# The second MLP's two products formed from seven block products each, in two stages with a*b kept in DRAM

## The chip, the cores and the metric

The kernel runs on one core of a Trainium2 chip. The metric is the device time of one execution in microseconds (us); lower is better. The engines are named as in the profile: PE (TensorE matmuls), PEld (its weight loads), DVE (VectorE), ACT (ScalarE), POOL (GpSimd), SP (the queue that issues the DMAs).

## The reference

Attention over 4 batches of 544 positions (32 global, 512 local, a window of 32) gives `x` with 2176 rows of 512. Two MLPs follow. This is the part that counts here:

```python
def _moe_ref(x, w_in, w_out):            # w_in 512 x 2048, w_out 2048 x 512
    h = np.maximum(x @ w_in, 0.0)
    return (h * h @ w_out).astype(np.float32)

def _moe2_ref(x, w1, w2, w3, w_out):     # w1, w2 512 x 1024, w3 1024 x 1024, w_out 1024 x 512
    a = x @ w1
    b = x @ w2
    h = a * b @ w3
    return (h @ w_out).astype(np.float32)
```

All arrays are float64 or float32 on the way in, and every matrix product has to be near float32 accuracy.

## The kernel before

**Products.** Activations lie with features on the 128 partitions and positions along the columns. A product near float32 is made of three passes of the reduced type `float32r`: an operand is split into a high part (a cast on ACT) and a low part (`raw - high`, `split_lo`, line 106), and `PASSES` multiplies high by high, high by low and low by high. So each raw operand tile costs one ACT instruction and one two-input DVE instruction before PE can use it. On DVE both inputs of `split_lo` lie in SBUF.

**Weights.** The inputs come as 64-bit floats, taken apart as integers. `conv(n)` makes unit n (128 x 512) of the 72: a 512 KB DMA (`load_w`), two ACT instructions (lines 373, 376), two DVE instructions (lines 381, 386), one POOL add (line 396), then the split. The calls `keep_in_program_order` hold the first ACT and the first DVE instruction of each unit at their place in the program.

**Order.** The text of the kernel is a program order. A planner with a model of the engines then fixes each engine's own order; a tile that has a tag and `bufs` waits for a free slot of that tag. `merge` spreads filler steps (the weights) between the main steps.

**Stages.** First attention with the first half of the first MLP, then its second half (`rows(NBLK + i, 16, 24, ...)`, eight blocks of 256 and 288 columns), with the weights of the second MLP as filler. In it `w_unit` also forms `w3 @ w_out` of the second MLP, kept in DRAM as `w_d`, so that the second MLP is `(a * b) @ w_d`. Its input `x2` is stored to DRAM (`x2_d`) block by block. The last stage is the second MLP: five blocks of columns, one of 256 and four of 480. For each block `p_unit` makes `a` and `b` for one of eight groups f of 128 features (24 matmuls), multiplies them (line 682) and splits the result at once; `x_add` adds group f's part to four accumulators (12 matmuls). A block so takes 8 x 36 = 288 matmuls; `end_c` copies the four results out and stores them.

Of the kernel before, what the change touches and what calls it, by code (L numbers as in the profile page):

```python
# [74 lines left out]
def attention_mlp(ctx: ExitStack, tc: tile.TileContext, kq0, kq, vw, wts, mask, ident, out):  # L75
# [569 lines left out]
    big = (NT - HALF) // 4
    blocks = [(0, HALF)] + [(HALF + big * k, big) for k in range(4)]
    x2, wv = {}, {}  # L650

    def load_x2(i):
        if i < len(blocks):
            s, n = blocks[i]
            x2[i] = sb.tile([128, 4, big], F32, tag="xb", name="x2l", bufs=2)[:, :, :n]
            nc.sync.dma_start(out=x2[i], in_=x2_d[:, :, s : s + n])

    def parts_c(n):
        return parts(n) if n <= NB else u2.tile([128, 2, big], F32R, tag="vb", name="hl_c", bufs=8)

    def split_x2(i, k):
        if i < len(blocks):
# [115 lines left out]
```

## Time and profile before

| | |
|---|---|
| device time, median of 3 runs | 901.23 us (900.71 to 902.02) |
| span of the profiled execution | 901.2 us |
| granted TensorE clock, mean over the span | 0.996 of full speed |
| PE busy | 869.4 us (96%) |
| DVE, ACT, POOL busy | 451.2, 473.7 and 164.8 us |
| HBM read and written | 71.63 and 19.92 MB |

The span is the time from the first to the last instruction of one profiled execution. "Busy" is the time in which an engine had an instruction running; PE's ends are modelled, so that rates of matmuls are better taken from how far apart their starts lie. POOL's busy time includes time in which it waits inside an instruction.

### The profile page before, as it was taken

To read this page: it belongs to the slowest core of one execution; us is meant where nothing else is said; L and a number is where in the kernel's file an instruction comes from. 1 tells how busy PE (TensorE), PEld (TensorE's weight loads), DVE (VectorE), ACT (ScalarE), POOL (GpSimd) and SP (SyncE) were. 2 spreads that over 40 slices of the span, in tenths; PEclk is the share of its full clock that TensorE was granted. 3 is DMA by queue.
4 is the path that set the end of the run, shared out by engine and by line. 5 is a ranking of instruction groups with operands and counts; after the bars stand their busy time and mean duration, and the time that the engine had idled before them with its cause. 6 is when DMAs were issued, how large, how long until landed. Compare 5 with 4: busy or idle time off the path is not lost.

```text
span 901.2 us, 15879 instructions
## 1 busy us (share of the span) xinstructions
PE 869.4 (96%) x6088; PEld 790.0 (88%) x6088; DVE 451.2 (50%) x1247; ACT 473.7 (53%) x1219; POOL 164.8 (18%) x182
## 2 busy tenths in 40 slices
PE   5798999999999999999999999999999999999998
PEld 3577898899999999999988999999988888888886
DVE  6998776876485455668545556753100200202101
ACT  5887675666476577878556576853111211212211
POOL 1442000000020022222222212211111111111111
PEclk9999999999999999999999999999999999999999
DMA  6653424313133055455353635544000200100101
GB/s 233 208 172 86 133 77 125 99 55 117 51 95 120 1 170 189 148 187 183 132 198 117 196 105 168 192 141 159 24 1 1 88 0 1 44 1 1 44 1 44
DMA packets 52348, 92.59 MB, mean 103 GB/s; under 512 B 4400, under 2 KB 35248, under 8 KB 52272
## 3 DMA queue, kind: packets, MB, share of 16 engines
q1 hardware_dynamic: 52272, 91.57, 30.9%
q8 instruction: 48, 0.79, 0.4%
q14 instruction: 28, 0.23, 0.1%
HBM read 71.63 MB, written 19.92 MB: 102 GB/s over the span
## 4 chain that ended last, share of the span: by engine, by line
PE 65%; DMA 13%; ACT 11%; DVE 8%; issue 2%; POOL 1%; SPq 1%; ACTq 0%; POOLq 0%; DVEq 0%
PE ab L117 21%; PE acc L468 14%; DMA wraw<-in_wts 12%; PE h L117 11%; PE x L117 8%; PE o L111 3%; PE sc L111 3%; ACT wt L373 3%; PE tp L265 3%; ACT wt L376 2%; DVE wt L386 2%; POOL wt L396 1%; PE sg L117 1%; ACT r L432 1%; DVE p L184 1%
## 5 line engine op out<-in xcount | busy, mean ns | idle before, releaser
L396 POOL TENSOR_TENSOR wt<-wt 128x512 int32<-128x512 int32 x72 | 97.4, 1352 | 294.8 <-DVE wt L386 214.0
L682 DVE TENSOR_TENSOR r<-r,ab 128x480 f32<-128x480 f32 (+1 forms) x40 | 24.3, 607 | 220.0 <-PE ab L117 219.2
L117 PE MATMUL h<-hl,ua 128*128 128x256 f32 (+1 forms) x768 | 120.1, 297 | 1.7 <-ACT hl L422 0.7
L117 PE MATMUL h<-hl,va 128*128 128x256 f32 (+1 forms) x768 | 111.0, 289 | 1.5 <-ACT r L432 1.4
L468 PE MATMUL acc<-hl,vb 128*128 128x256 f32 (+1 forms) x768 | 110.7, 289 | 1.7 <-DVE hl L106 1.6
L117 PEld LDWEIGHTS h<-hl,ua 128*128 128x128 f32 x768 | 103.4, 190 | 7.1 <-issue 1.7
L468 PEld LDWEIGHTS acc<-hl,vb 128*128 128x128 f32 x768 | 102.4, 188 | 4.2 <-DVE hl L106 2.2
L117 PEld LDWEIGHTS h<-hl,va 128*128 128x128 f32 x768 | 102.3, 188 | 3.4 <-ACT r L432 2.4
L117 PE MATMUL x<-hl,ub 128*128 128x288 f32 (+1 forms) x576 | 89.9, 296 | 1.4 <-ACT ub L397 1.2
L468 PE MATMUL acc<-hl_c,wv 128*128 128x480 f32 x384 | 89.2, 380 | 0.0
L117 PE MATMUL ab<-hl_c,ua 128*128 128x480 f32 x384 | 87.1, 380 | 0.0
L117 PE MATMUL ab<-hl_c,ub 128*128 128x480 f32 x384 | 86.6, 380 | 0.0
L117 PEld LDWEIGHTS ab<-hl_c,ub 128*128 128x128 f32 x384 | 72.0, 188 | 11.9
L117 PEld LDWEIGHTS ab<-hl_c,ua 128*128 128x128 f32 x384 | 71.9, 188 | 11.9
L117 PEld LDWEIGHTS x<-hl,ub 128*128 128x128 f32 x576 | 77.1, 189 | 5.8 <-issue 2.5
L468 PEld LDWEIGHTS acc<-hl_c,wv 128*128 128x128 f32 x384 | 72.1, 188 | 11.3
L681 ACT COPY r<-ab 128x480 f32<-128x480 f32 (+1 forms) x40 | 20.9, 523 | 116.2 <-PE ab L117 113.9
L106 DVE TENSOR_TENSOR hl<-r,hl 128x288 fp32r<-128x288 f32 (+1 forms) x128 | 69.6, 547 | 21.1 <-ACT r L439 19.9
L373 ACT ACTIVATE wt<-wraw 128x512 f32<-128x512 f32 x72 | 48.5, 675 | 58.8 <-DMA wraw<-in_wts 55.4
L106 POOL TENSOR_TENSOR hl_c<-r,hl_c 128x480 fp32r<-128x480 f32 x32 | 39.2, 1225 | 210.7 <-ACT hl_c L684 203.0
L188 ACT ACTIVATE p<-p,st 128x256 f32<-128x256 f32 x128 | 64.4, 509 | 7.0 <-DVE st L184 6.9
L684 ACT CAST hl_c<-r 128x480 fp32r<-128x480 f32 x32 | 19.0, 594 | 84.3 <-DVE r L682 84.3
(92 smaller groups left out, 1313.4 us busy)
## 6 DMA issues: line engine op xcount, KB each, us to landing
wraw<-in_wts SPq DMA_DIRECT2D x72, 512.0 KB, 3.4
v_f<-in_vw SPq DMA_DIRECT2D x24, 256.0 KB, 2.8
x2l<-x_d SPq DMA_DIRECT2D x4, 960.0 KB, 5.7
out<-y SPq DMA_DIRECT2D x16, 240.0 KB, 2.3
kqraw<-in_kq SPq DMA_DIRECT2D x24, 144.0 KB, 2.9
x_d<-xb SPq DMA_DIRECT2D x4, 576.0 KB, 6.0
part_d<-st SPq DMA_DIRECT2D x4, 576.0 KB, 3.3
xl<-x_d SPq DMA_DIRECT2D x4, 576.0 KB, 5.4
```

The source lines that it names most:

```text
L106: eng.tensor_tensor(out=lo, in0=raw, in1=hi.bitcast(F32), op=ALU.subtract)
L111: m = mm(o, w, x, start=start, stop=stop)
L117: mm(o, w, x, start=(k == 0), stop=(k == len(terms) - 1))
L188: nc.scalar.activation(p[:, n, :], p[:, n, :], AF.Exp, bias=least[:, n : n + 1], scale=-1.0, accum_out=sums[:, n, 0:1],)
L265: nc.tensor.transpose(tp[:, k, :], p[:, t % 2, 128 * half : 128 * (half + 1)], ident_sb)
L373: first = nc.scalar.activation(t[0].bitcast(F32), raw[:, :, 1].bitcast(F32), AF.Copy, scale=2.0**-112)
L376: nc.scalar.activation(t[2], raw[:, :, 0].bitcast(U32), AF.Copy, scale=2.0**-29)
L396: nc.gpsimd.tensor_tensor(out=b, in0=b, in1=m, op=ALU.add)
L468: mm(acc[d], w[:, a, 128 * d : 128 * (d + 1)], g_t[f][:, b], start=(f + k == 0), stop=(f + k == 9),)
L681: nc.scalar.copy(r, a)
L682: nc.vector.tensor_tensor(out=r, in0=r, in1=b, op=ALU.mult)
L684: nc.scalar.copy(g[:, 0], r)
```

## The change

The columns are cut into four panels p of 544 (two halves of `NP` = 272). A product of 2 x 2 blocks is made of seven block products in place of eight, with sums and differences of blocks formed before and after (Strassen's algorithm in Winograd's form). `ORDER` is the order of the seven, `BANK` the accumulator of each: 7 is added onto 6, 2 onto 1, 3 onto 5.

For `a` and `b` the blocks of the weights are w1 and w2 by halves of the 512 input features, those of the other operand are halves of the features by halves of the columns. `combine` makes the seven weight operands of a group f: four POOL sums of 256 columns and three and a half splits. `operands` makes those of a panel: four POOL sums of 544 elements for each raw tile, and 14 splits of 272 columns (28 for the second product). `Blocks.step` runs one product and what evacuates it: a copy on ACT and DVE sums that read PSUM. `ab_unit` is one panel and group: 7 x 6 matmuls of 272 columns, one DVE and one POOL multiplication, and a store of a*b to `r_d` in DRAM.

When all four panels have been through this, the second stage loads `r_d` panel by panel: two raw tiles, in the two slots of tag `xb`, by four DMAs. `y_unit` runs 7 x 12 matmuls of 272 columns for one of two pairs of output groups. The operands of panel p + 1 are made between the products of panel p.

Sixteen slots `u1` and sixteen `u2` take the place of the old tags. Groups f 0 to 3 lie in `u1` and are made in the first MLP's last stage; the weights of f 4 to 7 (`conv` 64 to 71, with their `combine`) are now made in the first 36 steps of the new stage. In the last panel the groups run in the order 4 to 7, 0 to 3, and the weights of the second product (`combine(("v", j), ...)`) are made beside the last four. `HL_BUFS` is 14 (13 before).

```diff
-UNITS = ["ua"] * 8 + ["ub"] * 8 + ["va"] * 8 + ["vb"] * 8 + ["ub"] * 8 + ["ua"] * 16 + ["ua"] * 8 + ["ub"] * 8
-
-RUNS = (0, 16, len(UNITS))
+UNITS = ["u1"] * 16 + ["u2"] * 16 + ["u1"] * 24
+PAIRED = len(UNITS)
+RUNS = (0, 16, PAIRED + 8, PAIRED + 16)
+
+
+
+ORDER = (1, 6, 5, 7, 4, 2, 3)
+BANK = {1: 0, 6: 1, 5: 2, 7: 1, 4: 3, 2: 0, 3: 2}
+NP = S // 2
...
-AT_BUFS, H_BUFS, X_BUFS, P_BUFS, KQ_BUFS, ST_BUFS = 4, 2, 2, 5, 4, 6
+AT_BUFS, H_BUFS, X_BUFS, P_BUFS, KQ_BUFS, ST_BUFS, HL_BUFS = 4, 2, 2, 5, 4, 6, 14
...
+    r_d = dram.tile([128, 8, NT], F32, name="r_d")
...
+    def unit(tag, dtype=F32R):
+        return pools[tag].tile([128, 2, 512], dtype, tag=tag, name=tag, bufs=16)
+
+    def split_w(t, cols, raw):
+        nc.scalar.copy(t[:, 0, cols], raw)
+        split_lo(nc.vector, t[:, 1, cols], raw, t[:, 0, cols])
+
+    blocks_w, both_t, half_t = {}, {}, {}
+
+    def combine(key, n, tag):
+
+        x = both_t.pop(key)
+        a11, a12, a21, a22 = (x[:, m, 256 * k : 256 * (k + 1)] for m in range(2) for k in range(2))
+        s = unit(tag, F32).rearrange("p a c -> p (a c)")
+        s1, s2, s3, s4 = (s[:, 256 * k : 256 * (k + 1)] for k in range(4))
+        p, q, r = (unit(tag) for _ in range(3))
+        add = nc.gpsimd.tensor_tensor
+        split_w(p, slice(0, 512), x[:, 0])
+        add(out=s1, in0=a21, in1=a22, op=ALU.add)
+        add(out=s2, in0=s1, in1=a11, op=ALU.subtract)
+        split_w(q, slice(0, 512), s[:, :512])
+        add(out=s3, in0=a11, in1=a21, op=ALU.subtract)
+        add(out=s4, in0=a12, in1=s2, op=ALU.subtract)
+        split_w(r, slice(0, 512), s[:, 512:])
+        if n % 2 == 0:
+            half_t[tag] = unit(tag)
+        h, at = half_t[tag], 256 * (n % 2)
+        split_w(h, slice(at, at + 256), a22)
+        blocks_w[key] = {1: (p, 0), 2: (p, 256), 5: (q, 0), 6: (q, 256), 7: (r, 0), 3: (r, 256), 4: (h, at)}
...
     def conv_c(n):
         _, b, m = mid_t.pop(n)
-        tag = UNITS[n]
-        t = pools[tag].tile([128, 2, 512], F32R, tag=tag, name=tag, bufs=8)
+        if n >= PAIRED:
+            f, u = divmod(n - PAIRED, 2)
+            tag = "u1" if f < 4 else "u2"
+            if u == 0:
+                both_t[f] = unit(tag, F32)
+            nc.gpsimd.tensor_tensor(out=both_t[f][:, u].bitcast(I32), in0=b, in1=m, op=ALU.add)
+            if u == 1:
+                combine(f, f, tag)
+            return
         nc.gpsimd.tensor_tensor(out=b, in0=b, in1=m, op=ALU.add)
...
+        t = w_t[n] = unit(UNITS[n])
+        split_w(t, slice(0, 512), b.bitcast(F32))
...
+    def banks():
+        return [
+            ps.tile([128, 512], F32, tag=tag, name="m", bufs=bufs)[:, :NP]
+            for tag, bufs in (("h", H_BUFS), ("at", AT_BUFS), ("at", AT_BUFS), ("x", X_BUFS))
+        ]
+
+    def temp():
+        return sb.tile([128, NB], F32, tag="tmp", name="r", bufs=4)[:, :NP]
+
+    def product(o, i, terms):
+        terms = [(w[:, a, c : c + 128], x[:, b]) for w, c, x in terms for a, b in PASSES]
+        for k, (w, x) in enumerate(terms):
+            mm(
+                o, w, x, start=(i in (1, 6, 5, 4) and k == 0), stop=(k == len(terms) - 1),
+                skip_group_check=(i in (2, 7, 3)),
+            )
+
...
+        def step(self, i):
+            if i == 1:
+                self.m = banks()
+            o, add = self.m[BANK[i]], nc.vector.tensor_tensor
+            product(o, i, self.terms(i))
+            if i == 1:
+                self.u = temp()
+                nc.scalar.copy(self.u, o)
+            elif i == 6:
+                self.u2 = temp()
+                add(out=self.u2, in0=self.u, in1=o, op=ALU.add)
+            elif i == 7:
+                add(out=self.u, in0=self.u, in1=o, op=ALU.add)
+                self.c22 = self.out(1, 1)
+                add(out=self.c22, in0=self.u, in1=self.m[2], op=ALU.add)
+            elif i == 4:
+                self.c21 = self.out(1, 0)
+                add(out=self.c21, in0=self.u, in1=o, op=ALU.subtract)
+            elif i == 3:
+                self.c12 = self.out(0, 1)
+                add(out=self.c12, in0=self.u2, in1=o, op=ALU.add)
+            self.done(self, i)
...
+    def operands(key, raws, scratch, tags):
+
+        b = lambda x, k, n: x[:, 2 * k : 2 * k + 2, NP * n : NP * (n + 1)]
+        ts = {}
+
+        def make(i):
+            out = xo[(*key, i)] = []
+            for q, x in enumerate(raws):
+                if i == 1:
+                    ts[q] = scratch(q)
+                    t1, t2 = ts[q]
+                    nc.gpsimd.tensor_tensor(out=t1, in0=b(x, 0, 1), in1=b(x, 0, 0), op=ALU.subtract)
+                    nc.gpsimd.tensor_tensor(out=t2, in0=b(x, 1, 1), in1=t1, op=ALU.subtract)
+                t1, t2 = ts[q]
+                if i == 7:
+                    nc.gpsimd.tensor_tensor(out=t1, in0=b(x, 1, 1), in1=b(x, 0, 1), op=ALU.subtract)
+                if i == 4:
+                    nc.gpsimd.tensor_tensor(out=t2, in0=t2, in1=b(x, 1, 0), op=ALU.subtract)
+                src = {1: b(x, 0, 0), 6: t2, 5: t1, 7: t1, 4: t2, 2: b(x, 1, 0), 3: b(x, 1, 1)}[i]
+                for k in range(2):
+                    t = parts(NP) if tags[i] == "hl" else unit(tags[i])[:, :, :NP]
+                    nc.scalar.copy(t[:, 0], src[:, k])
+                    split_lo(nc.vector, t[:, 1], src[:, k], t[:, 0])
+                    out.append(t)
+
+        return {i: lambda i=i: make(i) for i in ORDER}
+
+    def in_staging(q):
+        t = sb.tile([128, 4, NB], F32, tag="st", name="t12", bufs=1)
+        return t[:, :2, :NP], t[:, 2:, :NP]
+
...
+    def ops_early(d):
+        if d == 0:
+            first_ops()
+        if d < 2:
+            ops[0][ORDER[d]]()
...
+            NBLK + i, 16, 24,
+            (lambda d, i=i: split_b(i + 1, d)) if i < NBLK - 1 else ops_early,
+            lambda d, i=i: end_b(i, d),
...
+    fill = [lambda n=n: conv(n) for n in range(34, PAIRED + 8)]
...
+    end = main.pop()
+    main += [lambda i=i: ops[0][i]() for i in ORDER[2:]] + [end]
+    merge(main, (late, 0, 12), (fill, 12, len(main) - 27))
...
+    def ab_unit(p, f):
+
+        def terms(i):
+            w, c = blocks_w[f][i]
+            return [(w, c + 128 * k, xo["x", p, i][k]) for k in range(2)]
+
+        tile_r = []
+
+        def out(m, n):
+            if (m, n) == (1, 1):
+                return temp()
+            if not tile_r:
+                tile_r.append(unit("u1", F32).rearrange("p a c -> p (a c)")[:, :S])
+            return tile_r[0][:, NP * n : NP * (n + 1)]
+
+        def done(u, i):
+            if i == 2:
+                nc.vector.tensor_tensor(out=u.c21, in0=u.c21, in1=u.m[0], op=ALU.mult)
+            if i == 3:
+                nc.gpsimd.tensor_tensor(out=u.c12, in0=u.c12, in1=u.c22, op=ALU.mult)
+                nc.sync.dma_start(out=r_d[:, f, S * p : S * (p + 1)], in_=tile_r[0])
+
+        return Blocks(terms, out, done)
...
+    def load_wv(j):
+        t = both_t["v", j] = unit("u2", F32)
+        for k in range(2):
+            nc.sync.dma_start(
+                out=t[:, :, 256 * k : 256 * (k + 1)],
+                in_=w_d[j + 4 * k].rearrange("p (m c) -> p m c", m=2),
             )
...
+    def load_r(p):
+        out = []
+        for q in range(2):
+            t = sb.tile([128, 4, S], F32, tag="xb", name="rl", bufs=2)
+            src = columns(r_d, p).rearrange("p (h j) n -> p h j n", h=2)
+            for h in range(2):
+                nc.sync.dma_start(out=t[:, 2 * h : 2 * h + 2], in_=src[:, h, 2 * q : 2 * q + 2])
+            out.append(t)
+        return out
+
+    def scratch_r(q):
+        return in_raw(q) if q else in_staging(q)
+
+    RTAGS = {i: "u1" if i in (1, 6, 5, 7) else "hl" for i in ORDER}
+
+    def next_r(p):
+        if p < B:
+            ops[B + p] = operands(("r", p), load_r(p), scratch_r, RTAGS)
+
+    def next_x(p):
+        if p < B:
+            ops[p] = operands(("x", p), [load_x2(p)], in_staging, HL)
+
+    load_w(PAIRED + 8)
+    load_w(PAIRED + 9)
+    main = []
+    for p in range(B):
+        order = range(8) if p < B - 1 else (4, 5, 6, 7, 0, 1, 2, 3)
+        for n, f in enumerate(order):
+            box = []
+            if n == 1:
+                main.append(lambda p=p: next_x(p + 1))
+            if p == B - 1 and n >= 4:
+                main.append(lambda j=n - 4: load_wv(j))
+                main.append(lambda j=n - 4: combine(("v", j), j, "u2"))
+            if p == B - 1 and n == 5:
+                main.append(lambda: next_r(0))
+                main.append(lambda: ops[B][1]())
+            if p == B - 1 and n == 7:
+                main.append(lambda: ops[B][6]())
+            for i in ORDER:
+                if i == 1:
+                    main.append(lambda box=box, p=p, f=f: (box.append(ab_unit(p, f)), box[0].step(1)))
+                else:
+                    main.append(lambda box=box, i=i: box[0].step(i))
+                if n == 7 and p + 1 < B:
+                    main.append(lambda p=p, i=i: ops[p + 1][i]())
+            if p == B - 1 and n == 7:
+                for i in ORDER[2:]:
+                    main.append(lambda i=i: ops[B][i]())
+    merge(main, ([lambda n=n: conv(n) for n in range(PAIRED + 8, PAIRED + 16)], 0, 36))
+
+
+    def y_unit(p, s):
+
+        def terms(i):
+            at = [(*blocks_w["v", j][i], xo["r", p, i][j]) for j in range(4)]
+            return [(w, c + 128 * s, x) for w, c, x in at]
+
+        y = {}
+
+        def out(m, n):
+            if m not in y:
+                y[m] = unit("u2", F32).rearrange("p a c -> p (a c)")[:, :S]
+            return y[m][:, NP * n : NP * (n + 1)]
+
+        def store(m):
+            nc.sync.dma_start(out=out_d[:, 2 * m + s, S * p : S * (p + 1)], in_=y[m])
+
+        def done(u, i):
+            if i == 4:
+                store(1)
+            if i == 2:
+                nc.scalar.copy(out(0, 0), u.m[0])
+            if i == 3:
+                store(0)
+
+        return Blocks(terms, out, done)
+
+    for p in range(B):
+        units = [y_unit(p, s) for s in range(2)]
+        for i in ORDER:
+            for u in units:
+                u.step(i)
+            if i == 1:
+                next_r(p + 1)
+            if p + 1 < B:
+                ops[B + p + 1][i]()
 
 
 # ---- launch: one core; the arrays laid out on the host, nothing computed there ----
```

## Rows read from the trace of the kernel before

**Rows 1.** The page: span, and busy time by engine.

```profile
span 901.2 us, 15879 instructions
PE 869.4 (96%) x6088; PEld 790.0 (88%) x6088; DVE 451.2 (50%) x1247; ACT 473.7 (53%) x1219; POOL 164.8 (18%) x182
```

**Rows 2.** Windows: busy us and (instructions) of each engine, then granted clock, DMA.

```profile
core 0: us, PE busy (x) PEld busy (x) DVE busy (x) ACT busy (x) POOL busy (x), PEclk, DMA share, GB/s
537.00:562.00 25.00, 25.00 (x192) 24.93 (x192) 15.77 (x32) 18.80 (x44) 6.44 (x6) 1.00 0.51 169
...
650.00:700.00 50.00, 50.00 (x231) 42.98 (x230) 4.58 (x7) 7.52 (x13) 8.58 (x7) 1.00 0.03 10
```

**Rows 3.** The chain that ended last, from 560 us on, by line.

```profile
by line: PE ab L117 55.8%; PE acc L468 31.5%; DMA wraw<-in_wts 3.9%; PE h L117 2.9%; ACT wt L373 0.8%; POOL wt L396 0.8%; issue 0.5%; ACT ub L397 0.5%; ACT wt L376 0.5%; DVE wt L386 0.4%; ACT hl L433 0.4%; DVE wt L381 0.4%; ACT r L439 0.4%;
```

**Rows 4.** Timeline of PE: start us, us, instructions merged (xcount).

```profile
562.62 1.23 PE L468 MATMUL acc<-hl,vb 128*128 128x288 f32 x8
563.68 2.23 PE L117 MATMUL h<-hl,va 128*128 128x256 f32 x17
...
626.98 2.99 PE L117 MATMUL ab<-hl,ub 128*128 128x256 f32 x24
629.81 1.58 PE L468 MATMUL acc<-hl,wv 128*128 128x256 f32 x12
```

**Rows 5.** Groups by shape, DVE and ACT: xcount | busy us, mean ns.

```profile
L682 DVE TENSOR_TENSOR r<-r,ab 128x480 f32<-128x480 f32 x32 | 20.9, 654 | 199.3 <-PE ab L117 199.3
L682 DVE TENSOR_TENSOR r<-r,ab 128x256 f32<-128x256 f32 x7 | 2.9, 418 | 16.8 <-PE ab L117 16.1 <-ACT r L681 0.7
L106 DVE TENSOR_TENSOR hl<-x2l,hl 128x256 fp32r<-128x256 f32 x4 | 1.4, 419 | 0.0
L106 DVE TENSOR_TENSOR hl<-r,hl 128x288 fp32r<-128x288 f32 x1 | 0.4, 449 | 0.0
L386 DVE SCALAR_TENSOR_TENSOR wt<-wraw,wt 128x512 int32<-128x512 int32 x38 | 26.2, 689 | 0.8
L381 DVE TENSOR_SCALAR wt<-wt 128x512 int32<-128x512 int32 x38 | 16.0, 421 | 11.0 <-ACT wt L373 11.0
L422 ACT CAST hl<-xl 128x288 fp32r<-128x288 f32 x12 | 5.1, 421 | 0.0
```

**Rows 6.** Groups by shape, POOL.

```profile
L396 POOL TENSOR_TENSOR wt<-wt 128x512 int32<-128x512 int32 x72 | 97.4, 1352 | 294.8 <-DVE wt L386 214.0 <-ACT wt L376 25.2 <-ACT hl L433 17.0
L106 POOL TENSOR_TENSOR hl_c<-r,hl_c 128x480 fp32r<-128x480 f32 x32 | 39.2, 1225 | 210.7 <-ACT hl_c L684 203.0 <-DMA out<-y 7.8
L106 POOL TENSOR_TENSOR hl<-r,hl 128x256 fp32r<-128x256 f32 x8 | 6.0, 752 | 45.5 <-ACT hl L684 45.5
```

**Rows 7.** Timeline of POOL at two places.

```profile
41.74 1.97 POOL L396 TENSOR_TENSOR wt<-wt 128x512 int32<-128x512 int32 x1 [1.45 <-DVE stg L238]
...
332.38 1.29 POOL L396 TENSOR_TENSOR wt<-wt 128x512 int32<-128x512 int32 x1 [4.14 <-ACT wt L376]
```

**Rows 8.** Timeline of DVE at the same two places.

```profile
42.16 0.41 DVE L106 TENSOR_TENSOR hl<-xb,hl 128x256 fp32r<-128x256 f32 x1
42.50 0.41 DVE L184 CUSTOM_DVE_ANT_0 p<-sc,mask_sb 128x256 f32<-128x256 f32 x1
...
332.61 1.35 DVE L106 TENSOR_TENSOR hl<-r,hl 128x256 fp32r<-128x256 f32 x1 [0.39 <-ACT r L439]
```

**Rows 9.** DMA issues: xcount, KB each, median us to landing.

```profile
xl<-x_d SPq DMA_DIRECT2D x4, 576.0 KB, 5.4
xl<-part_d SPq DMA_DIRECT2D x4, 576.0 KB, 6.5
```

**Rows 10.** Timeline of SP: two loads issued one behind the other.

```profile
540.60 0.64 SPq L565 DMA_DIRECT2D xl<-x_d  x1
541.28 0.92 SPq L566 DMA_DIRECT2D xl<-part_d  x1
```

More of the change, by code (lines that the diff above doesn't have):

```diff
@@ new lines, in attention_mlp, with __init__ @@
+    class Blocks:
+        def __init__(self, terms, out, done):
+            self.terms, self.out, self.done = terms, out, done
+        def step(self, i):
[20 more added lines that the diff above has]
+            self.done(self, i)
@@ new lines, in in_staging, with in_raw, columns, load_x2 @@
+    def in_staging(q):
+        t = sb.tile([128, 4, NB], F32, tag="st", name="t12", bufs=1)
+        return t[:, :2, :NP], t[:, 2:, :NP]
+    def in_raw(q):
+        return [
+            pools["cv"].tile([128, 1024], F32, tag="wraw", name="t12", bufs=2)[:, : 2 * NP].rearrange(
+                "p (k n) -> p k n", k=2
+            )
+            for _ in range(2)
+        ]
+    def columns(t, p):
+        return t[:, :, S * p : S * (p + 1)]
+    def load_x2(p):
+        t = sb.tile([128, 4, S], F32, tag="xb", name="x2l", bufs=2)
+        nc.sync.dma_start(out=t, in_=columns(x2_d, p))
+        return t
@@ L632, in attention_mlp, with first_ops @@
+    HL = {i: "hl" for i in ORDER}
+    ops = {}
+    def first_ops():
+        ops[0] = operands(("x", 0), [load_x2(0)], in_raw, HL)
+    def ops_early(d):
[3 more added lines that the diff above has]
+            ops[0][ORDER[d]]()
     load_x(1)
@@ L648, in attention_mlp @@
[L648 to L662, printed above, removed]
-            t = xh[i, k] = parts_c(blocks[i][1])
-            nc.scalar.copy(t[:, 0], x2[i][:, k])
-            split_lo(nc.vector, t[:, 1], x2[i][:, k], t[:, 0])
@@ L667, in line @@
-    def line(name, k):
-        return pools["cv"].tile([128, 512], F32, tag=f"wt{k}", name=name, bufs=2)
-    def p_unit(i, f):
-        n = blocks[i][1]
-        a = ps.tile([128, 512], F32, tag="h", name="ab", bufs=H_BUFS)[:, :n]
-        b = ps.tile([128, 512], F32, tag="x", name="ab", bufs=X_BUFS)[:, :n]
-        for u, o in enumerate((a, b)):
-            w = w_t[56 + 2 * f + u]
-            chain(
-                o,
-                [(w[:, p, 128 * k : 128 * (k + 1)], xh[i, k][:, q]) for k in range(4) for p, q in PASSES],
-            )
-        r = line("r", 0)[:, :n]
-        nc.scalar.copy(r, a)
-        nc.vector.tensor_tensor(out=r, in0=r, in1=b, op=ALU.mult)
-        g = g_t[f] = parts_c(n)
-        nc.scalar.copy(g[:, 0], r)
-        split_lo(nc.gpsimd, g[:, 1], r, g[:, 0])
@@ L706, in attention_mlp @@
-    load_x2(0)
-    load_x2(1)
-    load_wv(0)
-    load_wv(1)
-    for k in range(4):
-        split_x2(0, k)
-    for i in range(len(blocks)):
-        for f in range(9):
-            if i == 0 and f < 8:
-                split_wv(f)
-            if f < 8:
-                p_unit(i, f)
-            if f == 7:
-                load_x2(i + 2)
-                for k in range(4):
-                    split_x2(i + 1, k)
-            if f > 0:
-                x_add(i, f - 1, wv[f - 1], blocks[i][1])
-        for d in range(4):
-            end_c(i, d)
+    end = main.pop()
```

31 lines of the change are left out of this document (5 added, 26 removed).

## Prediction

> **What bounds the kernel now.** I read the page first, then the windows by stage, then the chain of waits, then the timeline of PE. The page says that PE is busy 96% of the span, DVE and ACT half, POOL a fifth [rows 1]. In the stage that the change replaces, 650 to 700 us, PE is busy all the time while DVE, ACT and POOL work 4.6, 7.5 and 8.6 of 50 us [rows 2]. The chain of waits agrees: from 560 us on, 87.3% of it is the two matmul lines of the second MLP [rows 3]. So this stage lasts as long as its matmuls, and three engines are nearly free in it. The stage ahead of it, where the new weight operands of groups 0 to 3 must be made, is fuller: DVE works 15.8 and ACT 18.8 of 25 us [rows 2].
>
> **The profiled execution** has a span of 901.2 us, the median of the runs is 901.23. The sum below is made against 901.2. A difference under 0.2% (1.8 us) counts as no change.
>
> **Matmuls.** How far apart do they start? 231 of 480 columns in 50 us is 0.2165 us each [rows 2]. 24 of 256 columns start at 626.98, the next group at 629.81: 0.118 us. Eight of 288: 562.62 to 563.68, 0.1325 us [rows 4]. Halfway lies 0.125 us for 272 columns; both neighbours scaled by their columns give 0.125 as well, so this price has no wide bounds. Per column a 272 costs only 2% more than a 480: cutting the columns smaller loses little. Before: 4 blocks x 288 x 0.2165 + 288 x 0.118 = 249.4 + 34.0 = 283.4 us. After: 4 panels x 8 groups x 42 = 1344, and 4 x 2 x 84 = 672, together 2016 x 0.125 = 252.0 us. The change takes **31.4 us** of matmuls away. The old splits on ACT and POOL that go away were hidden under PE, so they give nothing.
>
> **What it adds, and the rule for sharing.** The new work is POOL sums and DVE splits, and these two exclude each other. At 332.61 a split of 256, normally 0.42 us [rows 5], took 1.35 us: it ended at 333.96, 0.29 us behind the POOL add that ran from 332.38 to 333.67 [rows 7, 8]. The other way round, the POOL add at 41.74 took 1.97 us and ended 1.14 us behind the split that ended at 42.57. A DVE instruction that reads PSUM, at 42.50, ran its usual 0.41 us inside that same add [rows 7, 8]. So two-input DVE work in SBUF and POOL sums go one after the other, and reading PSUM is free of it.
>
> The Trainium skill, "SBUF — State Buffer", section Terms, states this of a port pair that DVE and GpSimd share: it is exclusive, and the loser is blocked for the whole instruction. By that, full durations would add up, and my terms for panel 0 and for the second stage would be about 4 and 7 us larger (estimate), a sum of 898 in place of 887. The rows show a little less than full exclusion, and I go by them.
>
> Prices from the rows: a split of 256 occupies DVE for 0.34 us from start to start (42.16 to 42.50), 0.07 less than its duration; with 0.03 for 16 columns more [rows 5], 272 is 0.36, and 512 is 0.62. POOL: 0.752 at 256 and 1.225 at 480 [rows 6], so 0.79 at 272 and 1.36 at 544; an add that waited ended 1.14 us behind the split, 0.15 less than the undisturbed 1.29 [rows 7], so they hold 0.60 (256), 0.64 (272) and 1.21 us (544).
>
> **Panel 0 of the first stage.** Units 64 to 71 and the operands of groups 4 to 7 are now made while PE runs this panel; the calls that hold conversions in program order keep them from starting earlier. A conversion: POOL 1.14 + DVE 0.35 + 0.62 = 2.1 us, x8 = 17. A `combine`: 4 x 0.60 on POOL + 3 x 0.62 + 0.35 on DVE = 4.6, x4 = 18.5. Multiplications of seven groups on POOL: 4.5. Together 40 us that cannot overlap. A group takes 42 x 0.125 = 5.25 us on PE, and group 7 needs its last new operands 39 us into the panel. Beside that DVE has six PSUM sums a group, 0.37 us each, 15.4 us for seven groups; while POOL runs they are free, at other times they add. Half of them: about 8. Stall near 1 + 8, less what PE's own lateness gives back: **+6 us**. Bounds: 0 (all beside POOL) to 16 (none).
>
> **Panel changes, three times.** The 14 `hl` slots hold exactly one panel's operands, so operand i of the next panel waits for product i of the last group. From then to its own use, 0.75 to 9.75 us, there are 9.0 us; the work is 14 x 0.36 + 4 x 1.21 = 9.9 us, with PSUM sums between. 1.5 us each, **+4.5**; bounds 0 to 9.
>
> **Second stage.** PE needs 84 x 2 x 0.125 = 21.0 us a panel. Operands: 28 x 0.36 + 8 x 1.21 = 19.8 us. This would just fit, were the raw data there. But `load_r` of panel p + 1 takes the two `xb` slots that panel p's last operand still reads, so load and operands follow one another in a ring. Two loads of 576 KB land 5.4 us and 0.68 + 6.5 = 7.2 us behind the first issue [rows 9, 10]; each further one adds 1.8, so four of 544 KB need about 10.3 us, the first raw tile some 3.4 less. In those 3.4 us the first tile's 3.2 us of work are done; 16.6 us remain, less half a microsecond of splits that read no raw tile at the end. The ring takes **26 us** a panel, against PE's 21. Some operands of panel 0 are made beside the first stage's end, as slots come free; I put its last raw read 4 us into the stage (0 to 8). Then panel 3's last operand is ready at 4 + 3 x 26 = 82 us, with up to 6 us of products behind it: 88, PE alone 84. With lost moments: **+5 us**. Bounds: 0 at a ring of 24; +32 in the rival below.
>
> **The stage ahead and the end of the first stage.** Four `combine`s are new beside the last eight units of filler, and four more in the last panel, 4.6 us each; the 192 matmuls of 537 to 562 us, at 0.125 each 24.0 of 25 us, show that PE already loses 4% there [rows 2]. **+2 us**, 0 to 6.
>
> **At nothing.** ACT: 28 casts of 0.41 us [rows 5] are 11.5 of 21 us, PE covers them; if ACT were late, it would show as DVE waiting. The 9 MB to `r_d` (32 stores of 272 KB) and as much back lie beside 250 us of matmuls; what is not covered is the ring above. The end has one PSUM read and a store behind the last matmul in both kernels.
>
> **Sum:** 901.2 - 31.4 + 6 + 4.5 + 5 + 2 = **887 us**.
>
> **Rivals.** *All of it hidden*, and only the matmuls count: 901.2 - 31.4 + 2 = 872. For it: three idle engines. Against: 40 us of exclusive work in 39 us. Chance 0.15.
>
> *Late accumulators.* Product 7 goes onto the bank of product 6, so it must wait until DVE has read that bank. Product 6's last matmul starts 0.875 us ahead; its result is there after about 0.28 (24 matmuls last 2.99 us, 0.16 beyond the next start [rows 4]), the DVE sum takes 0.44 (between 418 and 654 ns [rows 5]): some 0.1 us is left. A split, or a split that waits for POOL, ahead of it in DVE's queue eats that. At 0.4 us late in each of 32 units, 32 x 0.3 = 10 us more: 897. Against: in panels 1 to 3 most units have no split beside them. Chance 0.13, range 893 to 903.
>
> *The ring is the bound*, and the kernel is slower. With full durations and PSUM sums that overlap nothing, a panel takes 10.3 + 28 x 0.43 + 8 x 1.36 + 10 x 0.43 - 3.4 = 34 us, and the stage 8 + 102 + 6 = 116 in place of 84: 914. It decides from 4 + 3 x ring + 6 = 103, a ring of 31 us; at 33, 907. For it: nothing but the four loads can fill the gap, since PE has no other work there. Against: the planner can split the operands that need no sum while POOL runs. Chance 0.22.
>
> **Chances.** Forecast 0.50, with its own range 878 to 896; hidden 0.15; late accumulators 0.13, half of it below 899.4; ring 0.22. Faster by over 0.2%: 0.50 + 0.15 + 0.06 = 0.71. Within: 0.06. Slower: 0.23, nearly all the ring's. The range 871 to 908 leaves out 1 in 10 on either side.
>
> **What would show it.** Matmuls of 272 columns 0.125 us apart. In the new stage PE idle in panel 0, mostly behind group 4, ended by DVE or ACT; then short stalls at each panel change; in the second stage one stall of some 5 us ahead of panels 2 and 3, ended by the loads of `r_d` or the first splits behind them. Splits of 272 that last over 1 us wherever POOL adds. I am wrong if the second stage shows no gap between panels, if panel 0 runs in 42 us, or if product 7 waits in every unit.

## The result: 0.8% slower, and the profile after

| | before | after |
|---|---|---|
| median of 4 runs each | 901.62 us (900.71 to 904.66) | 909.74 us (906.31 to 910.84) |
| ratio, 95% interval | 1 | 1.008 [1.0055, 1.0105] |
| span of the profiled execution | 901.2 us | 904.3 us |
| granted TensorE clock, mean | 0.996 | 0.984 |

The prediction, 887 us and faster, was wrong. The time lies 1.7 us above the upper end of its range. The profiled execution of the new kernel took 906.31 us, the shortest of the four. The account below explains its span, 3.1 us above that of before; the 3.4 us by which the median lies above it stand in no trace.

The page of the new kernel: span and busy times, the granted clock in 40 slices (9 is 90% of full speed or more), and the largest group of matmuls.

```profile
span 904.3 us, 17817 instructions
PE 853.4 (94%) x6664; PEld 802.5 (89%) x6664; DVE 623.1 (69%) x1601; ACT 505.4 (56%) x1349; POOL 257.4 (28%) x270
...
PEclk9889999999999999999999999999999999999989
...
L687 PE MATMUL m<-hl,u 128*128 128x272 f32 x1632 | 220.3, 294 | 18.3 <-DVE r L709 4.3
```

Against [rows 1], PE is busy 16 us less in a span 3 us longer, DVE 172 us more and POOL 93 us more. L687 is the matmul line of all block products; 1632 of the 2016 are in this group. The windows, one for a panel, two of the first stage and all four of the second, show where PE waits (columns as in [rows 2]):

```profile
core 0: us, PE busy (x) PEld busy (x) DVE busy (x) ACT busy (x) POOL busy (x), PEclk, DMA share, GB/s
603.00:662.00 59.00, 49.92 (x352) 46.44 (x351) 48.55 (x93) 26.16 (x54) 37.12 (x36) 0.97 0.47 161
662.00:710.00 48.00, 45.17 (x340) 44.04 (x340) 30.13 (x68) 9.88 (x27) 12.46 (x13) 0.96 0.19 67
...
801.00:826.00 25.00, 22.30 (x172) 21.43 (x172) 21.68 (x43) 11.70 (x35) 13.95 (x11) 1.00 0.35 126
826.00:851.00 25.00, 22.76 (x170) 22.40 (x169) 23.47 (x42) 11.84 (x36) 13.69 (x10) 0.93 0.40 144
851.00:880.00 29.00, 24.17 (x171) 23.70 (x170) 26.51 (x48) 14.64 (x44) 14.44 (x10) 0.88 0.32 114
880.00:901.00 21.00, 20.71 (x167) 20.49 (x166) 8.29 (x22) 2.53 (x7) 0.00 (x0) 1.00 0.17 63
```

The last panel has no operands to make for a panel behind it, and POOL does nothing: 21 us. The three ahead of it take 25, 25 and 29 us for the same products, with DVE busy 87 to 94%.

**The account.** "Lost" below is the time from the first matmul start of a stretch to the first of the next, less the number of matmuls times their undisturbed spacing: 0.125 us for 272 columns, the commonest distance of two starts in the new kernel as well as the forecast one, and 0.118, 0.132, 0.2165 and 0.2285 us for 256, 288, 480 and 512. A difference of 0.2 us between two of these figures means nothing.

| us | predicted | after |
|---|---|---|
| matmuls, 2016 x 0.125 in place of 283.4 | -31.4 | -31.4 |
| first stage, panel 0 | +6 | 15.2 lost |
| its panels 1 to 3 (for the panel changes) | +4.5 | 5.6 + 3.8 + 3.3 = 12.7 lost |
| second stage, panels 0 to 3 | +5 | 3.7 + 4.0 + 8.1 - 0.2 = 15.6 lost |
| stage ahead (from 390 us on) | +2 | 1.9 lost, before 6.7: -4.8 |
| lost in the old second MLP | 0 | -1.9 |
| after the last matmul start | 0 | 3.9, before 4.7: -0.8 |
| sum | -13.9 | +4.6 |

The spans differ by 3.1; the other 1.5 us lie outside these stretches. So the gain was there in full, and 43.5 us lost in the two stages took it back, of which 15.5 had been expected. The stretches don't cut quite as the terms of the prediction do: the end of panel 0 holds a part of the first panel change, and panel 3 the four `combine`s of the second product.

PE's waits from 600 us to the end, as what waited, for what, us in total, times, longest:

```profile
engine line waited for: us in total, times, longest us
PE m L687 <- DVE r L707: 8.8, 5, 3.8
PE m L687 <- DVE r L709: 4.3, 6, 1.4
PE m L687 <- DVE u L113: 3.0, 3, 2.0
PE m L687 <- DVE r L711: 2.6, 2, 1.6
PE m L687 <- DVE u L711: 2.3, 2, 1.4
PE m L687 <- ACT u L403: 1.8, 2, 1.1
PE m L687 <- DVE hl L113: 1.5, 3, 0.9
PE m L687 <- ACT r L704: 1.0, 1, 1.0
```

L707, L709 and L711 are DVE sums that read PSUM, the memory of PE's accumulators, and so free the bank that a later product starts on or is added to; they are called PSUM sums below. They ended 18.0 us. L113, the split that makes an operand, ended 4.5 us. PE waits four times as long for banks to be emptied as for operands to be made. ACT ended 2.8 us, so these are 25 of the 43.5 us. A granted clock below 1 explains at most 0.03 x 59 + 0.04 x 48 + 0.07 x 25 + 0.12 x 29 = 8.9 us more (it was 1.00 from 710 to 801 us): behind a wait some matmuls run at the lower of the two levels, 1.2 GHz. What is left, at least 9 us, must lie in gaps too short to be listed as waits (under 0.15 us).

The largest wait, around 863 us, read side by side. PE, DVE, POOL and the issues of SP:

```profile
860.89 1.75 PE L687 MATMUL m<-u,u 128*128 128x272 f32 x12 [1.01 <-DVE r L707]
866.46 3.09 PE L687 MATMUL m<-u,u 128*128 128x272 f32 x12 [3.83 <-DVE r L707]
869.35 10.53 PE L687 MATMUL m<-hl,u 128*128 128x272 f32 x72
...
863.29 2.77 DVE L113 TENSOR_TENSOR u<-rl,u 128x272 fp32r<-128x272 f32 x2 [2.46 <-ACT u L743]
865.99 0.42 DVE L707 TENSOR_TENSOR r<-r,m 128x272 f32<-128x272 f32 x1
...
862.92 1.34 POOL L733 TENSOR_TENSOR t<-rl 128x544 f32<-128x544 f32 x1 [8.36 <-DMA rl<-r_d]
864.34 1.42 POOL L734 TENSOR_TENSOR t<-rl,t 128x544 f32<-128x544 f32 x1
...
835.93 2.07 SPq L841 DMA_DIRECT2D rl<-r_d  x4
858.58 2.20 SPq L841 DMA_DIRECT2D rl<-r_d  x4
```

PE stands 3.83 us for one PSUM sum that takes 0.42. That sum stands in DVE's queue behind two splits of the next panel's first tile. They first wait 2.46 us for their raw data and then last 2.77 us together, because POOL adds at the same time. The load they wait for was issued at 858.58 and belongs to the next panel: PE needs neither split yet. So three things meet here: the order of DVE's queue, a late load and POOL's sums. The 12 matmuls behind the wait start 0.241 us apart (866.46 to 869.35) in place of 0.125, which adds 1.4 us.

### The profile page after: what moved, and what is told of

The parts are those of the page before. It is cut to its first block, busy times and chain, and to the rows that moved or that the text cites. A ratio compares the mean times of both kernels' runs of the same rounds, so it can differ in the third digit from the quotient of the medians.

```text
span 904.3 us, 17817 instructions
## 1 busy us (share of the span) xinstructions
PE 853.4 (94%) x6664; PEld 802.5 (89%) x6664; DVE 623.1 (69%) x1601; ACT 505.4 (56%) x1349; POOL 257.4 (28%) x270
## 4 chain that ended last, share of the span: by engine, by line
PE 64%; DVE 16%; DMA 7%; ACT 5%; issue 3%; POOL 3%; SPq 1%; DVEq 0%; ACTq 0%; POOLq 0%
PE m L687 16%; PE h L124 15%; PE acc L511 8%; PE x L124 8%; PE wacc L656 5%; DMA wraw<-in_wts 5%; DVE hl L113 4%; DVE u L113 4%; PE o L118 3%; PE sc L118 3%; PE tp L272 3%; DVE wt L393 2%; DMA rl<-r_d 2%; DVE p L191 1%; PE sg L124 1%
## 5 line engine op out<-in xcount | busy, mean ns | idle before, releaser
L687 PE MATMUL m<-hl,u 128*128 128x272 f32 x1632 | 220.3, 294 | 18.3 <-DVE r L709 4.3
L687 PEld LDWEIGHTS m<-hl,u 128*128 128x128 f32 x1632 | 211.7, 192 | 25.6 <-issue 4.3
L124 PE MATMUL h<-hl,u 128*128 128x288 f32 (+1 forms) x1536 | 230.2, 293 | 2.1 <-DVE r L478 0.7
L124 PEld LDWEIGHTS h<-hl,u 128*128 128x128 f32 x1536 | 205.6, 190 | 8.8 <-issue 2.5
L511 PE MATMUL acc<-hl,u 128*128 128x256 f32 (+1 forms) x960 | 137.5, 288 | 0.4 <-DVE hl L113 0.4
L511 PEld LDWEIGHTS acc<-hl,u 128*128 128x128 f32 x960 | 127.9, 188 | 1.8 <-DVE hl L113 0.6
L113 DVE TENSOR_TENSOR hl<-r,hl 128x288 fp32r<-128x288 f32 (+1 forms) x128 | 68.0, 535 | 40.0 <-ACT r L482 39.6
L124 PE MATMUL x<-hl,u 128*128 128x288 f32 (+1 forms) x576 | 89.9, 296 | 0.2 <-DVE hl L113 0.2
L124 PEld LDWEIGHTS x<-hl,u 128*128 128x128 f32 x576 | 77.1, 188 | 4.7 <-issue 2.5
L113 DVE TENSOR_TENSOR u<-wt,u 128x512 fp32r<-128x512 f32 x56 | 39.9, 713 | 33.7 <-ACT u L403 33.0
L687 PE MATMUL m<-u,u 128*128 128x272 f32 x384 | 53.5, 298 | 7.5 <-DVE r L707 7.1
L687 PEld LDWEIGHTS m<-u,u 128*128 128x128 f32 x384 | 51.2, 198 | 8.7 <-DVE r L707 5.3
L191 DVE CUSTOM_DVE_ANT_0 p<-sc,mask_sb 128x256 f32<-128x256 f32 x128 | 46.8, 418 | 13.0 <-PE sc L118 12.7
L476 ACT ACTIVATE hl<-r 128x288 fp32r<-128x288 f32 (+1 forms) x128 | 54.3, 430 | 2.2
L393 DVE SCALAR_TENSOR_TENSOR wt<-wraw,wt 128x512 int32<-128x512 int32 x72 | 54.1, 754 | 1.2
```

The costliest lines, as they stand in the source:

```text
L113: eng.tensor_tensor(out=lo, in0=raw, in1=hi.bitcast(F32), op=ALU.subtract)
L124: mm(o, w, x, start=(k == 0), stop=(k == len(terms) - 1))
L191: nc.vector.tensor_tensor_reduce(out=p[:, n, :], in0=sc[:, n, :], in1=mask_sb[:, 2 * part + n, :], scale=-SCALE, scalar=3.0e38, op0=ALU.ad ...
L393: nc.vector.scalar_tensor_tensor(out=b, in0=raw[:, :, 1], scalar=-(1 << 31), in1=a, op0=ALU.bitwise_and, op1=ALU.bitwise_or)
L476: nc.scalar.activation(g[:, 0], r, AF.Square)
L511: mm(acc[d], w[:, a, 128 * d : 128 * (d + 1)], g_t[f][:, b], start=(f + k == 0), stop=(f + k == 9),)
```

## The experiments

**Theories.** *Exclusion and queue* ("theory" in the expectations): POOL sums block DVE's splits, and DVE's PSUM sums, on which PE's fixed order waits, stand behind them in the order that DVE keeps. *Ring* (rival A): the second stage waits for its loads. *Late accumulators* (rival B): product 7 waits in each unit. *Slow link* (rival C): a POOL sum of 1.4 us is merely too slow a step in the making of an operand, with no exclusion needed. *Conversions* (in rival A too): panel 0 is short of DVE and POOL time for units 64 to 71. "As before" or "after" in an expectation is the changed kernel where it speaks of its parts. Each experiment is the changed kernel with one edit, and ratios are to the kernel before the change.

**All operand sums on DVE** (label e2_sums_dve): in `operands` and `combine`,

```diff
-        add = nc.gpsimd.tensor_tensor
+        add = nc.vector.tensor_tensor
...
-                    nc.gpsimd.tensor_tensor(out=t1, in0=b(x, 0, 1), in1=b(x, 0, 0), op=ALU.subtract)
+                    nc.vector.tensor_tensor(out=t1, in0=b(x, 0, 1), in1=b(x, 0, 0), op=ALU.subtract)
```

and so for the other sums.

> All operand sums (of panels and of weights) go from POOL to DVE; POOL keeps the conversions' adds and the multiplications. Theory (POOL sums block DVE's splits, and the PSUM sums queued behind those splits come late for PE): splits return to 0.43 us, the 45 us that PE loses over the eight panels fall to about 20, time near 884. Rival A (the ring of loads and the conversions in panel 0 are the bound, whoever makes the sums): 5 us less, near 904. Rival B (one product between 6 and 7 is too little for any loaded DVE): DVE has more in its queue, 905 to 912.

Measured: 890.58 us, 0.9859 [0.9841, 0.9877]. The fuller engine makes the sums too, and the kernel is 19 us faster than with the work shared out; some 26 had been expected. Its page, and its groups in the second stage (xcount | busy us, mean ns | idle ahead), then the same groups of the changed kernel:

```profile
PE 844.3 (95%) x6664; PEld 797.3 (90%) x6664; DVE 620.3 (70%) x1697; ACT 504.0 (57%) x1349; POOL 153.4 (17%) x174
...
L113 DVE TENSOR_TENSOR u<-t,u 128x272 fp32r<-128x272 f32 x44 | 16.5, 432 | 0.0
L113 DVE TENSOR_TENSOR u<-rl,u 128x272 fp32r<-128x272 f32 x12 | 4.8, 433 | 0.0
...
L734 DVE TENSOR_TENSOR t<-rl,t 128x544 f32<-128x544 f32 x6 | 4.3, 719 | 0.0
```

```profile
L113 DVE TENSOR_TENSOR u<-t,u 128x272 fp32r<-128x272 f32 x45 | 28.0, 664 | 1.4 <-ACT u L743 1.4
L113 DVE TENSOR_TENSOR u<-rl,u 128x272 fp32r<-128x272 f32 x12 | 15.2, 1298 | 5.5 <-ACT u L743 5.5
...
L113 DVE TENSOR_TENSOR hl<-rl,hl 128x272 fp32r<-128x272 f32 x32 | 12.2, 429 | 0.0
...
L707 DVE TENSOR_TENSOR r<-r,m 128x272 f32<-128x272 f32 x8 | 3.4, 429 | 1.7 <-PE m L687 1.0 <-issue 0.3 <-POOL u L821 0.3
...
L737 POOL TENSOR_TENSOR t<-rl 128x544 f32<-128x544 f32 x8 | 11.7, 1463 | 2.3 <-DVE u L113 2.3
```

Two groups of splits took 1298 and 664 ns on average in the changed kernel and 433 here; a third (`hl<-rl`) and the PSUM sums took 429 there too. Taken one by one from 600 us on, the changed kernel's 69 splits of 272 that overlapped a POOL instruction averaged 1004 ns and its 95 others 430; of its PSUM sums, 77 that overlapped one averaged 430 ns and 123 others 433. A sum of 544 takes DVE 0.72 us and POOL 1.46. DVE has 96 more instructions and is busy 2.8 us less: the added work is no more than the time that it had spent blocked. In the second stage PE now has a panel without any loss, beside a DVE that is busy 88% of it (columns as in [rows 2]):

```profile
823.00:844.00 21.00, 21.00 (x172) 21.00 (x171) 18.43 (x47) 10.12 (x31) 0.00 (x0) 1.00 0.43 155
```

The second stage lost 15.6 us and now 3.6, panels 1 to 3 of the first 12.7 and now 9.6, but panel 0 still 14.8. The edit also gives DVE another order, since the planner sees other work; e6 below keeps the order.

**Only the second stage's sums on DVE** (e10_r_only), the key deciding the engine: `add_on = nc.vector if key[0] == "r" else nc.gpsimd`.

> The changed kernel with the sums of the second stage's operands alone on DVE; sums of the first stage's operands and of the weights stay on POOL. Theory: the second stage loses 3 to 4 us in place of 16, the first stage its 28 as before, time 895 to 899, so two thirds of what e2_sums_dve won. If the exclusion in the first stage counts as much, the second stage's part is under 8 us and the time over 901.

Measured: 897.03 us, 0.9945 [0.9918, 0.9972]; 2.9 us lost in the second stage, 29.6 in the first, where the changed kernel lost 27.9. So two thirds of the gain of e2 come from the second stage.

**Panels' sums on DVE, weights' on POOL** (e7_mixed): the second half of the diff of e2.

> Sums of panels on DVE, sums of weights (combine) on POOL as in the changed kernel. The second stage as in e2_sums_dve, 3.6 us lost. Panel 0: if DVE's own load is what fills it there (17.6 of 21 us), less on DVE helps, 12 us lost in place of 15, time 888; if it is POOL's sums, 15 to 17 lost, 890 to 894.

Measured: 890.31 us, 0.9863 [0.9833, 0.9893], the same as e2. Where the weights' sums are done doesn't matter to the median; where the panels' sums are does. Its profiled execution, 885.4, was its shortest by 4 us and lost 11.4 us in panel 0, so whether panel 0 gains a little by it is open.

**e2 with POOL sums that nobody reads** (e6_dummy): beside each raw tile's operands POOL forms five subtractions of 432 elements into a spare tile.

```diff
+                for _ in range({1: 2, 7: 2, 4: 1}.get(i, 0)):
+                    nc.gpsimd.tensor_tensor(out=spare, in0=b(x, 0, 1)[:, :, :216], in1=b(x, 0, 0)[:, :, :216], op=ALU.subtract)
```

> As e2_sums_dve, all sums on DVE, but POOL makes idle subtractions of about the same total size beside them (five of 432 elements for each raw tile in place of four of 544; nobody reads their result). Theory (POOL and DVE's splits exclude each other): splits last over a microsecond again, the second stage loses 10 to 15 us in place of 3.6, time 899 to 905. Rival C (the sums on POOL were only slow links, 1.36 in place of 0.7 us, in the chain from raw tile to operand): no change, 889 to 893.

Measured: 925.08 us, 1.0263 [1.0238, 1.0288], 34 us above e2. Its groups in the second stage:

```profile
L113 DVE TENSOR_TENSOR u<-rl,u 128x272 fp32r<-128x272 f32 x12 | 13.4, 1151 | 0.0
L734 DVE TENSOR_TENSOR t<-rl,t 128x544 f32<-128x544 f32 x6 | 9.4, 1565 | 0.0
...
L707 DVE TENSOR_TENSOR r<-r,m 128x272 f32<-128x272 f32 x8 | 3.5, 437 | 0.3 <-POOL u L825 0.3
...
L737 POOL TENSOR_TENSOR spare<-rl 128x432 bf16<-128x432 f32 x30 | 38.5, 1282 | 34.2 <-DMA rl<-r_d 32.1
```

In this stage no operand depends on POOL, and the splits `u<-rl` are at 1151 ns again. By line and tile, PE's order is that of e2 in both stages, and so is DVE's from 671 us of e2's trace (684 of this one) to the end, 392 instructions; the loads of `r_d` wait for a DVE split in both. So the 18 us that the second stage loses more than in e2 (21.7 and 3.6) come from the POOL sums and not from another order or a longer ring. This shows the exclusion and refutes the slow link as what it takes. It cost more than expected; DVE's own sums, 719 ns in e2, are blocked too (1565). In the first stage the test is less clean, since the adds of the conversions and the multiplications stand behind the unread sums on POOL. The Trainium skill, "SBUF — State Buffer", sections Terms and "SBUF: two separate sides", names a port pair that DVE and GpSimd share, and says that a DVE instruction contends for it when it has two SBUF inputs and the GpSimd one reads SBUF, or in a two-port performance mode. The trace agrees: the splits, with two SBUF inputs, took 1151 to 1298 ns, the PSUM sums, with one, 429 to 437.

**No ring** (e3_no_ring): the raw tiles of panel 0 serve all four panels.

```diff
+        if p:
+            return raw_r
```

> Second stage without its ring: the raw tiles of panel 0 are loaded once and serve all four panels (the loads of panels 1 to 3 are left out, so the output is that of panel 0's a*b). Rival A: the second stage loses 2 us instead of 16, time near 895. Theory: the waits for the loads go (some 6 us), the blocked splits stay, near 903. Rival B: no change, 907 to 910.

Measured: 908.3 us, 1.0061 [1.0041, 1.008]: the same as with the loads, 15.0 us lost in the second stage. The ring isn't needed for the loss. Its largest wait shows the queue without any load in it, PE, then DVE, then POOL:

```profile
855.80 2.99 PE L687 MATMUL m<-hl,u 128*128 128x272 f32 x12 [5.14 <-DVE u L711]
...
840.75 1.49 DVE L113 TENSOR_TENSOR u<-rl,u 128x272 fp32r<-128x272 f32 x4
842.16 0.77 DVE L707 TENSOR_TENSOR r<-r,m 128x272 f32<-128x272 f32 x2
845.40 7.08 DVE L113 TENSOR_TENSOR u<-t,u 128x272 fp32r<-128x272 f32 x8 [2.47 <-ACT u L743]
852.41 1.94 DVE L113 TENSOR_TENSOR hl<-t,hl 128x272 fp32r<-128x272 f32 x2
854.27 0.42 DVE L709 TENSOR_TENSOR r<-r,m 128x272 f32<-128x272 f32 x1
854.62 0.78 DVE L113 TENSOR_TENSOR hl<-t,hl 128x272 fp32r<-128x272 f32 x2
855.32 0.43 DVE L711 TENSOR_TENSOR u<-r,m 128x272 f32<-128x272 f32 x1
...
839.57 3.91 POOL L733 TENSOR_TENSOR t<-rl 128x544 f32<-128x544 f32 x1 [2.90 <-DVE u L113]
```

Ten splits in 8.95 us stand between two PSUM sums; ten at e2's 433 ns would be about half of that. First DVE idled 2.47 us, because the tile that the splits need was late, and it was late because POOL's sum at 839.57 took 3.91 us beside DVE's row of splits.

**No conversions in panel 0** (e4_no_conv): groups 4 to 7 use the operands of groups 0 to 3 (`blocks_w[f % 4][i]`), and units 64 to 71 with their `combine` are left out.

> Panel 0 without the weights of groups 4 to 7: groups 4 to 7 use the operands of groups 0 to 3, and the eight conversions and four combines in panel 0 are left out. Theory and rival A: panel 0 loses 3 to 5 us instead of 17, time near 896. Rival B: panel 0 loses 10 or more, near 903, since DVE still makes its sums one product ahead of PE.

Measured: 899.63 us, 0.9964 [0.9949, 0.9978]; panel 0 lost 9.0 in place of 15.2 us, between the two forecasts.

**Both** (e8_sums_noconv): e2 and e4 together.

> e2_sums_dve without the conversions and combines of groups 4 to 7 in panel 0 (left out; these groups use the operands of groups 0 to 3). If the conversions fill panel 0, it loses 3 to 5 us in place of 15, time 878 to 881. If panel 0's loss is that of its start (first operands late), 9 us stay, near 885.

Measured: 877.83 us, 0.9738 [0.9719, 0.9757]; panel 0 lost 4.4. Against the changed kernel, leaving out the conversions alone gives 10 us, moving the sums 19, both 32: two causes that roughly add up.

**Product 7 one place later** (e5_order4): a whole product more lies between 6 and 7, and the sum of c21 moves with it.

```diff
-ORDER = (1, 6, 5, 7, 4, 2, 3)
+ORDER = (1, 6, 5, 4, 7, 2, 3)
```

> Product 4 goes ahead of product 7, so two products stand between 6 and the one that is added onto its bank; the work is the same. Rival B: the waits for the first DVE sum go (10 us of those over 0.2 us), and more in small ones, time 890 to 897. Theory: a split that is blocked for over a microsecond still stands ahead of the sums, the waits move to the next sum, 903 to 908. Rival A: no change.

Measured: 909.76 us, 1.0068 [1.0048, 1.0088]: no change, 1.8 us above what the theory expected. In the second stage the waits moved on: those that L707 ended fell from 7.1 us to 0.6, those that L711 ended, two sums later, rose from 2.3 to 8.4. Product 7 as the one place where PE waits is refuted.

**e2 with four of the eight conversions earlier** (e9_early), two `combine`s with them, in the last block of the first MLP; the scratch of panel 0's operands moves to the staging tile for it:

```diff
+    more = [lambda n=n: conv(n) for n in range(PAIRED + 8, PAIRED + 12)]
...
-    merge(main, (late, 0, 12), (fill, 12, len(main) - 27))
+    merge(main, (late, 0, 12), (fill, 12, len(main) - 27), (more, len(main) - 27, len(main)))
```

The remaining four run over the first 20 steps of panel 0.

> e2_sums_dve, with four of the eight conversions and two of the four combines of panel 0 moved ahead into the last block of the first MLP, and the scratch of panel 0's operands in the staging tile. If the conversions fill panel 0, its loss falls by about half, 7 to 8 us, for 2 us in the stage ahead: 884 to 886. If not, 889 to 893.

Measured: 883.78 us, 0.982 [0.9788, 0.9852]; panel 0 lost 8.0 in place of 14.8 us, the stage ahead 4.9 in place of 2.7. Moving the work paid more than it cost there.

**e9 with the weights' sums on POOL** (e12_mixed_early).

> e9_early with the sums of weights on POOL. Theory: as e9_early within 3 us, 882 to 888, since these sums lie where conversions' adds are on POOL anyway.

Measured: 884.72 us, 0.9807 [0.9776, 0.9838], the same as e9, as e7 is the same as e2.

**e9 with the multiplication a*b on DVE too** (e11_early_mult): line 821 on `nc.vector`.

> e9_early with the first stage's multiplication of c12 and c22 on DVE as well, so that POOL has only the conversions' adds left. Theory: 32 x 0.64 us of blocking become 32 x 0.36 us of DVE work, 1 to 3 us less, 880 to 883. If DVE's own load decides, no better than e9_early, 883 to 887.

Measured: 879.81 us, 0.9759 [0.9721, 0.9797]: 2.4% faster than the kernel before the change, and the fastest of those that leave nothing out. A window with as many matmuls (x352) as that of the changed kernel from 603 us on:

```profile
603.00:655.00 52.00, 47.28 (x352) 44.75 (x351) 48.49 (x109) 22.14 (x51) 7.90 (x6) 1.00 0.40 138
```

POOL's 37 us of the changed kernel are 8 here. DVE has 16 instructions more and the same 48.5 us, and the window is 7 us shorter. This much e9 had won already: its panel 0 lost 8.0 us, that of e11 8.1. Of the 3.9 us by which the profiled execution is shorter than that of e9, 3.1 lie in the second stage, which begins beside the last multiplications.

**e11 with six conversions earlier** (e13_early6).

> e11_early_mult with six of the eight late conversions moved ahead. If room in the last block of the first MLP is left, panel 0 loses 2 to 4 us less, 878 to 881. If the slots of u2, still held by the first MLP's weights, bound it, no change or worse, 882 to 886.

Measured: 883.31 us, 0.9796 [0.9769, 0.9822]: no better, 0.4% above e11, whose slowest run took 883.29; panel 0 lost 12.8 us where e11 lost 8.1. PE's longest wait there, 3.66 us, ended with a PSUM sum that stood on DVE behind two sums for the next panel, two instructions of conversions and a multiplication; the multiplication and the second sum took 1.50 and 1.78 us, beside two conversions' adds on POOL. Whether the slots of the new operands or the denser order of the last two conversions did it wasn't tried.

The time lost (us), by stretch, in the profiled executions:

| | stage ahead | first stage, panels 0 to 3 | second stage | span |
|---|---|---|---|---|
| changed kernel | 1.9 | 15.2, 5.6, 3.8, 3.3 | 15.6 | 904.3 |
| e3, no ring | 3.6 | 15.7, 4.8, 3.9, 3.6 | 15.0 | 906.3 |
| e5, product 7 later | 2.7 | 17.2, 3.9, 3.1, 3.8 | 18.3 | 907.8 |
| e4, no conversions | 4.2 | 9.0, 3.8, 3.7, 2.2 | 15.8 | 898.6 |
| e2, sums on DVE | 2.7 | 14.8, 3.9, 1.7, 4.0 | 3.6 | 889.0 |
| e10, second stage's sums on DVE | 2.0 | 16.9, 4.9, 3.9, 4.0 | 2.9 | 895.3 |
| e7, panels' sums on DVE | 2.1 | 11.4, 4.0, 1.8, 3.1 | 1.6 | 883.6 |
| e6, e2 + unread POOL sums | 5.1 | 18.5, 10.3, 2.1, 7.1 | 21.7 | 923.6 |
| e9, e2 + four earlier | 4.9 | 8.0, 1.7, 1.7, 3.7 | 3.2 | 881.6 |
| e11, e9 + product on DVE | 4.4 | 8.1, 1.1, 1.1, 3.6 | 0.1 | 877.7 |
| e8, sums + no conversions | 3.3 | 4.4, 1.6, 1.6, 1.7 | 2.9 | 875.3 |

## Why the prediction was wrong, point by point

**Matmuls, -31.4: right.** The spacing of 272 columns is the forecast 0.125 us, and the last panel of the second stage ran its 168 matmuls in 20.8 us of the forecast 21.0.

**The exclusion: right as a mechanism.** Splits beside POOL sums lasted 1298 ns and PSUM sums kept their 0.43 us, as [rows 7, 8] had suggested; e6 shows it alone. One price was read wrongly on the way: 0.03 us lies between 256 and 288 columns in [rows 5], so 16 columns more are 0.015; the 0.36 that the sum uses is right.

**Second stage, +5: the step that failed,** with 15.6. Not the ring: its loads of panels 2 and 3 were issued 22.65 us apart (835.93 and 858.58), shorter than the forecast 26, and left out in e3 they changed nothing. The last split of operands ended at 883.8 us, 83 us into the stage, where 82 was forecast. What failed is the clause behind it, "up to 6 us of products behind it": at 883.8 PE still had 16.7 us of matmuls to do (to 900.5).

```profile
879.71 10.56 PE L687 MATMUL m<-u,u 128*128 128x272 f32 x84
...
882.97 0.78 DVE L113 TENSOR_TENSOR hl<-rl,hl 128x272 fp32r<-128x272 f32 x2
```

The sum priced the exclusion as throughput, as if PE could run all older products while DVE made operands. But those products need PSUM sums from DVE, and they stand in its queue among the blocked splits. PE therefore lost its time while panels 0 to 2 ran, at products 7 and 3, and no gap opened between the panels, which was the prediction's own first sign of being wrong. Taking the POOL sums out of that stage (e10) returned 12.7 us of it.

**Panel 0, +6: mis-sized,** 15.2 lost. The prediction counted 40 us of exclusive work and half of the PSUM sums, and set the 39 us until group 7 against them. Half of the panel's loss, 6 to 7 us, goes when the conversions go (e4) or four of them go elsewhere (e9); the sums' engine alone changes nothing there (e2), the two together leave 4.4 (e8). So conversions and sums together fill the panel, and "half of them" was too little. That they cost PE its time by the same queue is likely, but no run shows it alone. The upper bound of 16, PSUM sums that overlap nothing, was near; the choice of "half of them" had no row behind it.

**Panel changes, +4.5: mis-sized,** 12.7. With the sums on DVE they lost 9.6 (e2), and with earlier conversions and the product on DVE as well 5.8 (e11), so exclusion and what panel 0 left late both seem to stand in them. In what shares is open.

**Stage ahead, +2: wrong sign,** -4.8. Eight conversions left it, and four `combine`s came. The prediction counted the `combine`s as an addition and nothing for what left. Putting four conversions back (e9) cost 2.2 us against e2. Kernels with no edit in that stage lost from 1.9 (changed kernel) to 4.2 us (e4), so 2.2 us is within that spread, and how much of the 4.8 is due to the conversions that left is open.

**Tail, ACT, DRAM traffic, 0: right.** The tail gave 0.8 us back. Of PE's waits, ACT ended 2.8 us, no DMA directly, and e3 gained nothing by leaving loads out.

**The rivals.** *All hidden* is refuted by 43.5 us lost. *The ring* gave a time near the measured one (907 to 914) for a reason that e3 refutes; by the number alone it would have won, by luck. *Late accumulators* had the right kind of wait, PE standing for a PSUM sum behind a split or a split behind POOL, but placed it at product 7 alone, which e5 refutes, and priced it at 10 us; the waits fall on several sums (L707, L709, L711), 18.0 us in all.

**What stays open:** how the waits divide between splits that are blocked, raw tiles that come late and the order in which DVE's queue was fixed, since a PSUM sum was never put ahead of the splits by itself; why e13 is worse than e11; and the 3.4 us between the profiled execution and the median.

## What to carry to other kernels

When work goes to engines "with idle time", ask what else stands in the same in-order queue: here a 0.42 us PSUM sum, late behind splits that nobody needed yet, stopped a PE that had all its operands. Where two engines exclude each other, add up how long the second one blocks the first: POOL took twice as long per sum as DVE and held DVE up meanwhile, so moving the sums to the fuller engine made it no busier and the kernel 2.1% faster than with them shared out. A saving in matmuls (31 us here) is only as good as the side work beside them; e11 keeps 22 of it.
